# Fourteen weight units of layer 2 converted to float32 during layer 1, through scratch in device memory; eight late activations for twelve

## The chip, the cores and the metric

The kernel runs on one NeuronCore of a Trainium2 chip. The metric is device time in microseconds (us) of one execution, the median of several runs. The engines are named as the profile names them: TensorE is PE (its weight loads PEld), VectorE is DVE, ScalarE is ACT, GpSimd is POOL, SyncE is SP; ACT, POOL and SP also issue transfers.

## What is computed

The reference takes float32 inputs: an attention block whose heads are mixed before and after the softmax, and two dense layers. Only the layers matter here.

```python
# x: 896 tokens x 768, from the attention block
h = x @ w1_in                                  # 768 -> 2048
x = (h * clip(h + 3, 0, 6) / 6) @ w1_out       # 2048 -> 768
h = x @ w2_in                                  # 768 -> 2048
P = a0 + a1*h + a2*h**2 + a3*h**3
Q = 1 + |b0|*|h| + |b1|*h**2
out = (P / (Q + 1e-6)) @ w2_out                # 2048 -> 768
```

The weights of the layers arrive as 64-bit floats and have to be turned into 32-bit ones on the chip.

## The kernel before

Attention comes first (until about 262 us of the span); it isn't touched. The layers then work on weight units, in the order of the list `units`: 16 units `in1` (128 of the 2048 columns each), 18 units `out1`, and for layer 2 16 units `in2` and 16 `out2`, interleaved with `out2` one pass behind.

`load_unit` (L380) issues the load of a unit from SP into a tile `wraw` (two buffers): 768 KB for most. `split_pieces` (L394) then works in two halves. The first turns the 64-bit words into a float32 tile `wf` (two buffers; for `out2` a part of the large tile `wo2`): one ACT instruction (L408) for the high words and three DVE instructions on integers (L410, L412, L416). The second cuts the float32 into two float32r parts, `wh` and `wl` (three buffers each): in layer 1 both on POOL (L423, L424), in layer 2 `wh` on ACT (L426) and `wl` on DVE (L427). Every product is three matmuls (`mm3`, L364 to L366): high by high, high by low, low by high.

`advance(i)` (L446) loads units up to i+2 and splits units up to i+1. The code below the attention is written in the order of the units, and a scheduler moves instructions within it, engine by engine; each engine then runs its own list strictly in order.

Layer 1: for each f, two matmul groups (384 and 512 tokens, the two PARTS) into PSUM banks (eight, in turn), and `act1` (L506) on ACT and DVE, which writes `gh` and `gl`; its temporaries are the tiles `tmp` (seven buffers). Then, for each of six output column blocks, three `out1` units.

Layer 2, the main loop over f: 18 matmuls of 384 tokens into bank h0, `act2` (L701) on them, then 18 of 512 tokens into bank h1. `act2` is five ACT and six DVE instructions (L707, L710 to L714); bank h0 or h1 is free once L711 has read it. For most f the second part is "late": a copy on ACT (L759) takes it out of the bank, and its activation follows in the tail. `late_f` (L736) names these: twelve, all but f = 3, 7, 11, 15. `gemm_out0` adds 18 matmuls for the 384 tokens, one pass behind.

The tail is the output product of the 512 tokens, 16 steps of 24 matmuls, in the order `order` (L777): first the f that are not late, then the late ones. `prep(i)` (L780) makes the operands of a step: `gs` from the activation (ACT, and L719 on DVE) and `ws` from `wo2` (ACT L789, DVE L790). At step i the code writes down prep(i+2) and then the i-th late activation.

Of the kernel before, what the change touches and what calls it, by code (L numbers as in the profile page):

```python
# [7 lines left out]
F32 = mybir.dt.float32  # L8
F32R = mybir.dt.float32r
I32 = mybir.dt.int32  # L10
# [39 lines left out]
def fused_kernel(  # L50
# [15 lines left out]
    nc = tc.nc  # L66
    NT, DM = out.shape
    DFF = w1_out.shape[0]
    WARM = 11
    KD = DM // 128  # L70
    KF = DFF // 128
# [20 lines left out]
    w1i = w1_in.bitcast(I32).rearrange("(c p) f -> p c f", p=128)  # L92
    w1o = w1_out.bitcast(I32).rearrange("(f p) c -> p f c", p=128)
    w2i = w2_in.bitcast(I32).rearrange("(c p) f -> p c f", p=128)

    xp = tc.alloc_tile_pool(name="xp", bufs=1)
    x1p = tc.alloc_tile_pool(name="x1p", bufs=1)
# [263 lines left out]
    pools = {}  # L361
# [17 lines left out]

    def load_unit(u, eng=nc.sync):  # L380
        kind, i, kk = u
        t = pools['late'].tile([128, KD * 256], I32, tag="wraw", bufs=2, name="wraw")
        cols = slice(i * 256, i * 256 + 256)
        if kind in ("in1", "in2"):
            src = (w1i if kind == "in1" else w2i)[:, :, cols]
        elif kind == "out1":
            src = w1o[:, KSP[kk][0] : KSP[kk][1], cols]
        else:
            src = w2_out.bitcast(I32)[i * 128 : i * 128 + 128, :].rearrange("p (a b) -> p a b", b=256)
        n = src.shape[1]  # L390
        eng.dma_start(out=t[:, : n * 256].rearrange("p (a b) -> p a b", b=256), in_=src)
        raws[u] = (t, n)

    def split_pieces(u):  # L394


        t, n = raws.pop(u)
        n *= 128
        tv = t[:, : 2 * n].rearrange("p (a two) -> p a two", two=2)
        hw, lw = tv[:, :, 1], tv[:, :, 0]  # L400
        if u[0] == "out2":
            if not wo2:
                wo2.append(pools["gp2"].tile([128, KF, DM], F32, name="wo2"))
            w = wo2[0][:, u[1], :]
        else:
            w = pools["late"].tile([128, KD * 128], F32, tag="wf", bufs=2, name="wf")[:, :n]
        wi = w.bitcast(I32)
        nc.scalar.activation(out=w, in_=hw.bitcast(F32), func=AF.Copy, scale=2.0**-112)  # L408
        yield
# [7 lines left out]
            out=wi, in0=lw, scalar=icst[:, 1:2], in1=wi, op0=ALU.logical_shift_right, op1=ALU.bitwise_or  # L417
        )
        yield
        hv = pools["late"].tile([128, KD * 128], F32R, tag="wh", bufs=3, name="wh")[:, :n]  # L420
        lv = pools["late"].tile([128, KD * 128], F32R, tag="wl", bufs=3, name="wl")[:, :n]
        if u[0] in ("in1", "out1"):
# [78 lines left out]
            pass  # L501

    def tmp(name, n):
        return pools["gp"].tile([128, 512], F32, tag="tmp", bufs=7, name=name)[:, :n]

    def act1(f, p):  # L506
        t0, t1 = PARTS[p]
# [151 lines left out]
        return pm.tile([128, 512], F32, tag="mm", name=name)  # L659


    ui = 2
    for f in range(2, KF):
        advance(ui)
        for p in range(2):
            run(gemm1(f, p, bank(f"h1_{f}_{p}")))
            act1(f, p)
        ui += 1
    for c in range(KD):
        hp = [bank(f"y1_{c}_{p}") for p in range(2)]  # L670
        for kk, (k0, k1) in enumerate(KSP):
            advance(ui)
            wh, wl = spl.pop(("out1", c, kk))
            for f in range(k0, k1):
                for p, (t0, t1) in enumerate(PARTS):
                    mm3(hp[p][:, : t1 - t0], wh[:, f - k0, :], wl[:, f - k0, :], gh[f][:, t0:t1], gl[f][:, t0:t1],
                        f == 0, f == KF - 1)
            ui += 1
        for p, (t0, t1) in enumerate(PARTS):
            y = tmp("y", t1 - t0)  # L680
            nc.scalar.activation(out=y, in_=hp[p][:, : t1 - t0], func=AF.Copy, scale=1.0 / 6.0)
            nc.vector.tensor_copy(out=XH[:, c, t0:t1], in_=y)
            nc.vector.tensor_tensor(out=XL[:, c, t0:t1], in0=y, in1=XH[:, c, t0:t1].bitcast(F32), op=ALU.subtract)
# [49 lines left out]

    acc0 = []
    g0, g1 = {}, {}
    late_f = [f for f in range(KF) if f % 4 != 3]  # L736

    def gemm_out0(f):
        w = spl.pop(("out2", f, 0))
# [137 lines left out]
```

## Time and profile before

| | |
|---|---|
| time, median of 3 runs | 751.38 us (749.64 to 752.59) |
| the profiled execution | 750.68 us |
| its span, first to last instruction | 749.0 us |
| PE busy | 715.0 us, 95% of the span |
| DVE busy | 533.2 us, 71% |
| ACT busy | 427.9 us, 57% |
| POOL busy | 258.0 us, 34% |
| mean clock granted to PE | 0.986 of full speed |

The times of single instructions come from one profiled execution. Its span leaves out 1.7 us around the first and the last instruction. A busy PE is not PE at its peak: matmuls overlap, and a wait shorter than a matmul's length shows in the distance between starts and not as idle time. So the starts of PE's rows are of more use than its busy share.

### The profile page before, as it was taken

How to read it: one execution, taken by the hardware profiler on the slowest of the kernel's cores; microseconds unless marked ns; L12 is line 12 of the kernel's file. 1: busy time of each engine (PE TensorE's matmuls, PEld its weight loads, DVE VectorE, ACT ScalarE, POOL GpSimd, SP SyncE). 2: the span in 40 equal slices, each digit the busy share in tenths (PEclk: the TensorE clock that was granted, in tenths of full speed). 3: DMA queues.
4: the chain of work that ended last, by engine and by line, in shares of the span. 5: the costliest groups of instructions: out<-in, count | busy, mean ns of one | idle time of the engine just before them, and what ended most of it. 6: DMA issues, size and time to landing. Idle time of an engine off the chain costs nothing.

```text
span 749.0 us, 12177 instructions
## 1 busy us (share of the span) xinstructions
PE 715.0 (95%) x4457; PEld 621.4 (83%) x4457; DVE 533.2 (71%) x947; ACT 427.9 (57%) x869; POOL 258.0 (34%) x255
## 2 busy tenths in 40 slices
PE   5799999999998999999999999999999998999986
PEld 3578777787886988888888888889998897999876
DVE  5554556555456489767635555589999999999996
ACT  4577677777678444343411111256766575789872
POOL 1676766676668535444344333200000000000000
PEclk8899999999999999999999999999999999999999
DMA  6535356445358325333233333324354443501002
GB/s 187 176 122 155 119 179 183 142 141 149 118 151 227 99 85 167 91 122 106 93 113 112 111 97 94 121 85 132 122 169 127 126 144 110 169 18 46 1 1 84
DMA packets 63283, 89.76 MB, mean 120 GB/s; under 512 B 5172, under 2 KB 53880, under 8 KB 63224
## 3 DMA queue, kind: packets, MB, share of 16 engines
q1 hardware_dynamic: 62592, 88.55, 38.4%
q8 instruction: 35, 0.57, 0.3%
q10 hardware_dynamic: 568, 0.43, 0.2%
q14 instruction: 24, 0.20, 0.1%
q0 software_dynamic: 64, 0.01, 0.1%
HBM read 66.87 MB, written 2.75 MB: 93 GB/s over the span
## 4 chain that ended last, share of the span: by engine, by line
PE 74%; DVE 15%; ACT 4%; DMA 4%; issue 2%; SPq 1%; POOL 0%; ACTq 0%; POOLq 0%; DVEq 0%
PE h L364 9%; PE h L366 9%; PE h L365 9%; PE A L320 8%; PE X L340 5%; PE y L364 5%; PE y L365 5%; PE y L366 5%; PE sc L254 5%; PE M L285 4%; PE M L287 2%; PE acc L365 2%; PE M L286 2%; PE acc L366 2%; PE acc L364 2%
## 5 line engine op out<-in xcount | busy, mean ns | idle before, releaser
L364 PE MATMUL h<-xh,wh 128*128 128x512 f32 (+1 forms) x384 | 142.6, 371 | 2.3 <-DVE u L711 1.3
L366 PE MATMUL h<-xh,wl 128*128 128x512 f32 (+1 forms) x384 | 141.5, 370 | 2.1 <-DVE wl L427 2.1
L365 PE MATMUL h<-xl,wh 128*128 128x512 f32 (+1 forms) x384 | 141.3, 368 | 0.0
L408 ACT ACTIVATE wf<-wraw 128x768 f32<-128x768 f32 (+1 forms) x50 | 43.7, 875 | 122.8 <-POOL wl L424 101.4
L275 POOL TENSOR_TENSOR sl<-full,sh 120x448 fp32r<-120x448 f32 x89 | 103.5, 1163 | 7.4
L289 DVE TENSOR_REDUCE st<-M 120x1 f32<-120x448 f32 x90 | 56.1, 623 | 68.0 <-PE M L287 63.9
L320 PEld LDWEIGHTS A<-wr,e 120*112 120x112 f32 x720 | 85.1, 176 | 19.6 <-ACT wr L304 16.1
L320 PE MATMUL A<-wr,e 120*112 120x120 f32 x720 | 90.3, 268 | 8.4 <-ACT wr L304 8.1
L291 ACT ACTIVATE e<-M,st 120x448 f32<-120x448 f32 x90 | 57.1, 635 | 60.6 <-DVE st L289 60.5
L364 PEld LDWEIGHTS h<-xh,wh 128*128 128x128 f32 x384 | 72.6, 189 | 12.2 <-DVE u L711 2.2
L366 PEld LDWEIGHTS h<-xh,wl 128*128 128x128 f32 x384 | 72.5, 189 | 11.8 <-DVE wl L427 3.3
L273 POOL TENSOR_SCALAR sh<-full 120x448 fp32r<-120x448 f32 x89 | 54.1, 607 | 77.3 <-PE M L286 43.0
L410 DVE TENSOR_SCALAR wf<-wf 128x768 int32<-128x768 int32 (+1 forms) x50 | 27.6, 551 | 74.2 <-ACT wf L408 74.0
L365 PEld LDWEIGHTS h<-xl,wh 128*128 128x128 f32 x384 | 72.7, 189 | 8.2
L423 POOL TENSOR_SCALAR wh<-wf 128x768 fp32r<-128x768 f32 (+1 forms) x34 | 33.4, 982 | 128.8 <-PE y L365 56.0
L364 PE MATMUL y<-gh,wh 128*128 128x384 f32 x192 | 70.6, 368 | 0.0
L365 PE MATMUL y<-gl,wh 128*128 128x384 f32 x192 | 70.2, 366 | 0.0
L366 PE MATMUL y<-gh,wl 128*128 128x384 f32 x192 | 69.7, 363 | 0.0
L424 POOL TENSOR_TENSOR wl<-wf,wh 128x768 fp32r<-128x768 f32 (+1 forms) x34 | 65.7, 1934 | 2.8
L324 ACT ACTIVATE at<-A 112x480 f32<-112x480 f32 x90 | 51.5, 572 | 2.8 <-PE A L320 2.8
L416 DVE SCALAR_TENSOR_TENSOR wf<-wraw,icst,wf 128x768 int32<-128x768 int32 (+1 forms) x50 | 51.3, 1028 | 0.8
L412 DVE SCALAR_TENSOR_TENSOR wf<-wraw,icst,wf 128x768 int32<-128x768 int32 (+1 forms) x50 | 50.6, 1012 | 0.8
(113 smaller groups left out, 1515.7 us busy)
## 6 DMA issues: line engine op xcount, KB each, us to landing
wraw<-in_moe_w_in_dram SPq DMA_DIRECT2D x32, 768.0 KB
wraw<-in_moe_w_out_dram SPq DMA_DIRECT2D x28, 768.0 KB
full<-stg SPq DMA_DIRECT2D x60, 210.0 KB
vraw<-in_v_dram SPq DMA_DIRECT2D x42, 224.0 KB
full<-stg SPq DMA_DIRECT2D x24, 157.5 KB
wraw<-in_moe_w_out_dram SPq DMA_DIRECT2D x6, 512.0 KB
kraw<-in_k_dram SPq DMA_DIRECT2D x6, 448.0 KB
qraw<-in_q_dram SPq DMA_DIRECT2D x6, 360.0 KB
```

What stands on the lines that cost most here:

```text
L273: eng.tensor_scalar(out=sh[:r], in0=s[:r], scalar1=1.0, scalar2=0.0, op0=ALU.mult, op1=ALU.add)
L275: return eng.tensor_tensor(out=sl[:r], in0=s[:r], in1=sh[:r].bitcast(F32), op=ALU.subtract)
L289: nc.vector.tensor_reduce(out=st[:r, 0:1], in_=mt[:r, :S], op=ALU.max, axis=AX.X, negate=True)
L291: nc.scalar.activation(out=e[:r], in_=mt[:r, :S], func=AF.Exp, bias=st[:r, 0:1], accum_out=st[:r, 1:2])
L320: nc.tensor.matmul(av[:, jc], lhsT=e[:r, jc * JP : (jc + 1) * JP], rhs=wr[:r, :, :rr], start=True, stop=True)
L324: lambda: nc.scalar.activation(out=at[C][:, :, :, c0 : c0 + rr], in_=av, func=AF.Copy)
L364: nc.tensor.matmul(o, lhsT=wh, rhs=mh, start=first, stop=False)
L365: nc.tensor.matmul(o, lhsT=wh, rhs=ml, start=False, stop=False)
L366: nc.tensor.matmul(o, lhsT=wl, rhs=mh, start=False, stop=last)
L412: nc.vector.scalar_tensor_tensor(out=wi, in0=hw, scalar=icst[:, 0:1], in1=wi, op0=ALU.bitwise_and, op1=ALU.bitwise_or)
L416: nc.vector.scalar_tensor_tensor(out=wi, in0=lw, scalar=icst[:, 1:2], in1=wi, op0=ALU.logical_shift_right, op1=ALU.bitwise_or)
L424: nc.gpsimd.tensor_tensor(out=lv, in0=w, in1=hv.bitcast(F32), op=ALU.subtract)
```

## The change

The units `in2` of f = 2 to 15 get their first half (`to_f32`, the same four instructions) during layer 1. A function `pre_slot` is called after each f of layer 1 and after each `out1` unit, 32 times. It takes two calls for a unit: the first loads the 64-bit unit into a tile `wpre` (one buffer), the second converts it into a `wf` buffer; the first call for the next unit, ahead of its own load, stores the `wf` to a scratch tensor `pre` in device memory. All these transfers are issued by SP. In layer 2 `load_unit` reads the float32 back (384 KB) straight into a `wf` buffer, and `split_pieces` only does its second half. The room for `wpre` comes from `tmp`, four buffers for seven. And `late_f` becomes the eight even f, so that eight second activations run in the loop where four did, and eight follow in the tail where twelve did. The order of the tail's steps changes with it: f = 1, 3, ... 15, then 0, 2, ... 14. Everything computed is the same.

```diff
@@ -92,6 +92,11 @@
+    PRE2 = list(range(2, KF))
+    dram = ctx.enter_context(tc.tile_pool(name="dram", bufs=1, space=bass.MemoryType.DRAM))
+    pre = {f: dram.tile([128, KD * 128], F32, name=f"pre{f}") for f in PRE2}
@@ -379,6 +384,11 @@
     def load_unit(u, eng=nc.sync):
         kind, i, kk = u
+        if kind == "in2" and i in pre:
+            t = pools["late"].tile([128, KD * 128], F32, tag="wf", bufs=2, name="wf")
+            eng.dma_start(out=t, in_=pre[i])
+            raws[u] = (t, KD)
+            return
@@ -391,19 +401,11 @@
-    def split_pieces(u):
...
+    def to_f32(t, n, w):
...
         wi = w.bitcast(I32)
         nc.scalar.activation(out=w, in_=hw.bitcast(F32), func=AF.Copy, scale=2.0**-112)
         yield
...
@@ -417,6 +419,20 @@
+    def split_pieces(u):
+        t, n = raws.pop(u)
+        n *= 128
+        if u[0] == "in2" and u[1] in pre:
+            w = t
+        else:
+            if u[0] == "out2":
+                if not wo2:
+                    wo2.append(pools["gp2"].tile([128, KF, DM], F32, name="wo2"))
+                w = wo2[0][:, u[1], :]
+            else:
+                w = pools["late"].tile([128, KD * 128], F32, tag="wf", bufs=2, name="wf")[:, :n]
+            yield from to_f32(t, n, w)
@@ -501,7 +517,7 @@
     def tmp(name, n):
-        return pools["gp"].tile([128, 512], F32, tag="tmp", bufs=7, name=name)[:, :n]
+        return pools["gp"].tile([128, 512], F32, tag="tmp", bufs=4, name=name)[:, :n]
@@ -659,12 +675,35 @@
+    slot, held = [0], {}
+
+    def pre_slot():
+        i, k = divmod(slot[0], 2)
+        slot[0] += 1
+        if k == 0 and 0 < i <= len(PRE2):
+            nc.sync.dma_start(out=pre[PRE2[i - 1]], in_=held["w"])
+        if i >= len(PRE2):
+            return
+        f = PRE2[i]
+        n = KD * 128
+        if k == 0:
+            held["t"] = gp.tile([128, 2 * n], I32, tag="wpre", name=f"wpre{f}")
+            nc.sync.dma_start(
+                out=held["t"].rearrange("p (a b) -> p a b", b=256), in_=w2i[:, :, f * 256 : f * 256 + 256]
+            )
+        else:
+            held["w"] = pools["late"].tile([128, n], F32, tag="wf", bufs=2, name="wf")
+            for _ in to_f32(held["t"], n, held["w"]):
+                pass
     ui = 2
     for f in range(2, KF):
         advance(ui)
         for p in range(2):
             run(gemm1(f, p, bank(f"h1_{f}_{p}")))
             act1(f, p)
+        pre_slot()
         ui += 1
...
+            pre_slot()
             ui += 1
@@ -733,7 +773,7 @@
-    late_f = [f for f in range(KF) if f % 4 != 3]
+    late_f = [f for f in range(KF) if f % 2 == 0]
```

The lists of the engines move at three places. The first is DVE in layer 1, around the activation of f=8. In the names, g1, t1, gh8 and gl8 belong to `act1`, h1_8_0 is the first matmul group of f=8, and wf is a unit under conversion. Before:

```order
L516 SCALAR_TENSOR_TENSOR g1_3952<-t1_3950,h1_8_0_3929 128x384
L416 SCALAR_TENSOR_TENSOR wf_4109<-wraw_4044,icst_68,wf_4109 128x768
L519 TENSOR_TENSOR gl8_3949<-g1_3952,gh8_3948 128x384
L516 SCALAR_TENSOR_TENSOR g1_3977<-t1_3975,h1_8_1_3956 128x512
L410 TENSOR_SCALAR wf_4172<-wf_4172 128x768
L519 TENSOR_TENSOR gl8_3949<-g1_3977,gh8_3948 128x512
L412 SCALAR_TENSOR_TENSOR wf_4172<-wraw_4107,icst_68,wf_4172 128x768
L516 SCALAR_TENSOR_TENSOR g1_4015<-t1_4013,h1_9_0_3992 128x384
L416 SCALAR_TENSOR_TENSOR wf_4172<-wraw_4107,icst_68,wf_4172 128x768
```

The same place with the change:

```order
L532 SCALAR_TENSOR_TENSOR g1_3991<-t1_3989,h1_8_0_3968 128x384
L418 SCALAR_TENSOR_TENSOR wf_4093<-wraw_4023,icst_68,wf_4093 128x768
L535 TENSOR_TENSOR gl8_3988<-g1_3991,gh8_3987 128x384
L412 TENSOR_SCALAR wf_4159<-wf_4159 128x768
L414 SCALAR_TENSOR_TENSOR wf_4159<-wraw_4091,icst_68,wf_4159 128x768
L418 SCALAR_TENSOR_TENSOR wf_4159<-wraw_4091,icst_68,wf_4159 128x768
L532 SCALAR_TENSOR_TENSOR g1_4016<-t1_4014,h1_8_1_3995 128x512
L412 TENSOR_SCALAR wf_4220<-wf_4220 128x768
L414 SCALAR_TENSOR_TENSOR wf_4220<-wpre6_4155,icst_68,wf_4220 128x768
L535 TENSOR_TENSOR gl8_3988<-g1_4016,gh8_3987 128x512
L532 SCALAR_TENSOR_TENSOR g1_4057<-t1_4055,h1_9_0_4034 128x384
L418 SCALAR_TENSOR_TENSOR wf_4220<-wpre6_4155,icst_68,wf_4220 128x768
```

The three instructions on wf_4220 are the unit f=6 of `in2`, converted from wpre; around it stand the activations and the conversions of layer 1's own units.

The second place is DVE in the loop of layer 2, at f=9. Here t1, y0, u and r belong to `act2`, g0l9 is the split of its result, wo2 a unit `out2` under conversion, h2_9_0 and h2_9_1 the contents of banks h0 and h1. Before:

```order
L713 SCALAR_TENSOR_TENSOR u_6193<-u_6193,pa_66,r_6196 128x384
L410 TENSOR_SCALAR wo2_5337<-wo2_5337 128x768
L714 SCALAR_TENSOR_TENSOR t1_6192<-y0_6194,u_6193 128x384
L427 TENSOR_TENSOR wl_6240<-wf_6234,wh_6239 128x768
L719 TENSOR_TENSOR g0l9_6209<-t1_6192,g0h9_6208 128x384
L412 SCALAR_TENSOR_TENSOR wo2_5337<-wraw_6232,icst_68,wo2_5337 128x768
L416 SCALAR_TENSOR_TENSOR wo2_5337<-wraw_6232,icst_68,wo2_5337 128x768
L410 TENSOR_SCALAR wf_6333<-wf_6333 128x768
L412 SCALAR_TENSOR_TENSOR wf_6333<-wraw_6261,icst_68,wf_6333 128x768
L427 TENSOR_TENSOR wl_6268<-wo2_5337,wh_6267 128x768
```

With the change:

```order
L751 SCALAR_TENSOR_TENSOR u_6309<-u_6309,pa_66,h2_9_0_6289 128x384
L412 TENSOR_SCALAR wo2_5465<-wo2_5465 128x768
L752 SCALAR_TENSOR_TENSOR y0_6310<-y0_6310,r_6312 128x384
L753 SCALAR_TENSOR_TENSOR u_6309<-u_6309,pa_66,r_6312 128x384
L414 SCALAR_TENSOR_TENSOR wo2_5465<-wraw_6658,icst_68,wo2_5465 128x768
L754 SCALAR_TENSOR_TENSOR t1_6308<-y0_6310,u_6309 128x384
L443 TENSOR_TENSOR wl_6393<-wo2_5465,wh_6392 128x768
L747 SCALAR_TENSOR_TENSOR y0_6348<-h2_6349,pb_67,y0_6348 128x512
L759 TENSOR_TENSOR g0l9_6325<-t1_6308,g0h9_6324 128x384
L750 TENSOR_TENSOR u_6347<-h2_9_1_6328,u_6347 128x512
L418 SCALAR_TENSOR_TENSOR wo2_5465<-wraw_6658,icst_68,wo2_5465 128x768
L751 SCALAR_TENSOR_TENSOR u_6347<-u_6347,pa_66,h2_9_1_6328 128x512
```

The conversion of wf is gone, and the second activation of f=9 (on h2_9_1, 512 columns) stands in its place; its third instruction, L751 on h2_9_1, is the one that frees bank h1.

The third place is DVE at the end of the late activations in the tail. The xl rows from wo2 and from g1 are the two DVE instructions of a preparation, the others the activation of f=13 and f=14. Before:

```order
L713 SCALAR_TENSOR_TENSOR u_7360<-u_7360,pa_66,r_7363 128x512
L790 TENSOR_TENSOR xl_85<-wo2_5337,xh_84 128x768
L714 SCALAR_TENSOR_TENSOR g1_13_6582<-y0_7361,u_7360 128x512
L707 SCALAR_TENSOR_TENSOR y0_7404<-h2_7405,pb_67,y0_7404 128x512
L710 TENSOR_TENSOR u_7403<-g1_14_6681,u_7403 128x512
L719 TENSOR_TENSOR xl_85<-g1_13_6582,xh_84 128x512
L711 SCALAR_TENSOR_TENSOR u_7403<-u_7403,pa_66,g1_14_6681 128x512
L712 SCALAR_TENSOR_TENSOR y0_7404<-y0_7404,r_7406 128x512
L713 SCALAR_TENSOR_TENSOR u_7403<-u_7403,pa_66,r_7406 128x512
L790 TENSOR_TENSOR xl_85<-wo2_5337,xh_84 128x768
L714 SCALAR_TENSOR_TENSOR g1_14_6681<-y0_7404,u_7403 128x512
```

With the change:

```order
L747 SCALAR_TENSOR_TENSOR y0_7346<-h2_7347,pb_67,y0_7346 128x512
L750 TENSOR_TENSOR u_7345<-g1_14_6800,u_7345 128x512
L759 TENSOR_TENSOR xl_101<-g1_4_5790,xh_100 128x512
L751 SCALAR_TENSOR_TENSOR u_7345<-u_7345,pa_66,g1_14_6800 128x512
L752 SCALAR_TENSOR_TENSOR y0_7346<-y0_7346,r_7348 128x512
L753 SCALAR_TENSOR_TENSOR u_7345<-u_7345,pa_66,r_7348 128x512
L830 TENSOR_TENSOR xl_101<-wo2_5465,xh_100 128x768
L754 SCALAR_TENSOR_TENSOR g1_14_6800<-y0_7346,u_7345 128x512
L759 TENSOR_TENSOR xl_101<-g1_6_5992,xh_100 128x512
L830 TENSOR_TENSOR xl_101<-wo2_5465,xh_100 128x768
```

Before, the last activation, of f=14, is interleaved with the preparation of step 14 (f=13). With the change it is interleaved with that of step 10 (f=4), and behind it stand preparations alone, the first of them that of step 11 (f=6).

PE's list keeps its order but for neighbours, and POOL's is the same. SP's list gains 14 loads into wpre and 14 stores of wf, each store directly ahead of the next wpre load and behind two loads of layer 1.

## Rows read from the trace of the kernel before

**Rows 1.** The page: engines over the whole span, and DVE by fortieths of it.

```profile
PE 715.0 (95%) x4457; PEld 621.4 (83%) x4457; DVE 533.2 (71%) x947; ACT 427.9 (57%) x869; POOL 258.0 (34%) x255
...
DVE  5554556555456489767635555589999999999996
```

**Rows 2.** Busy time by stretch: us, then PE, PEld, DVE, ACT, POOL, PEclk, DMA, GB/s.

```profile
262.00:380.00 118.00, 118.00 (x573) 104.33 (x573) 90.67 (x118) 51.00 (x83) 50.20 (x32) 1.00 0.36 110
380.00:492.00 112.00, 112.00 (x552) 99.98 (x551) 57.22 (x72) 20.59 (x29) 40.90 (x30) 1.00 0.35 110
492.00:669.00 177.00, 172.64 (x868) 156.80 (x867) 170.16 (x258) 119.17 (x194) 0.00 (x0) 0.99 0.39 121
669.00:745.00 76.00, 70.82 (x384) 67.43 (x382) 72.03 (x110) 57.81 (x95) 0.00 (x0) 0.98 0.08 31
```

**Rows 3.** Timeline of PE: first matmuls of f=0, 4, 7 and of the tail.

```profile
492.27 0.34 PE L364 MATMUL h<-xh,wh 128*128 128x384 f32 x1
...
542.07 0.34 PE L364 MATMUL h<-xh,wh 128*128 128x384 f32 x1
...
573.71 0.34 PE L364 MATMUL h<-xh,wh 128*128 128x384 f32 x1
...
668.80 0.51 PE L364 MATMUL acc<-xh 128*128 128x384 f32 x2
```

**Rows 4.** Waits of PE, loop (492 to 669), then tail: total, times, longest.

```profile
PE h L366 <- DVE wl L427: 2.1, 2, 1.6
PE h L364 <- DVE u L711: 1.3, 2, 1.0
...
PE acc L365 <- DVE xl L790: 4.1, 3, 2.2
```

**Rows 5.** Groups of DVE by shape, 492 to 745: busy us, mean ns, idle before.

```profile
L416 DVE SCALAR_TENSOR_TENSOR wo<-wraw,icst,wo 128x768 int32<-128x768 int32 x16 | 16.2, 1014 | 0.1
...
L707 DVE SCALAR_TENSOR_TENSOR y<-h,pb,y 128x512 f32<-128x512 f32 x16 | 11.9, 745 | 0.0
L712 DVE SCALAR_TENSOR_TENSOR y<-y,r 128x512 f32<-128x512 f32 x16 | 11.0, 685 | 0.1
...
L410 DVE TENSOR_SCALAR wo<-wo 128x768 int32<-128x768 int32 x16 | 8.9, 554 | 0.2 <-ACT wo L408 0.2
```

**Rows 6.** Timeline of DVE in the tail: L707 rows two steps apart.

```profile
695.68 0.74 DVE L707 SCALAR_TENSOR_TENSOR y<-h,pb,y 128x512 f32<-128x512 f32 x1
...
706.22 0.74 DVE L707 SCALAR_TENSOR_TENSOR y<-h,pb,y 128x512 f32<-128x512 f32 x1
```

**Rows 7.** Timeline of DVE in the tail: preparation 3's end, and the last copy.

```profile
677.15 0.95 DVE L790 TENSOR_TENSOR xl<-wo,xh 128x768 fp32r<-128x768 f32 x1
...
745.11 0.56 DVE L730 COPY o<-acc 128x384 f32<-128x384 f32 x1 [1.24 <-PE acc L366]
```

**Rows 8.** Waits of POOL, 262 to 492: total us, times, longest.

```profile
POOL wh L423 <- PE y L365: 56.0, 15, 5.0
POOL wh L423 <- PE h L365: 52.2, 13, 4.4
```

**Rows 9.** Timeline of POOL in layer 1: one unit's split.

```profile
301.35 1.40 POOL L423 TENSOR_SCALAR wh<-wf 128x768 fp32r<-128x768 f32 x1 [4.02 <-PE h L365]
302.83 2.04 POOL L424 TENSOR_TENSOR wl<-wf,wh 128x768 fp32r<-128x768 f32 x1
```

**Rows 10.** Timeline: a load issued by SP, and ACT's first use of it.

```profile
497.31 0.37 SPq L391 DMA_DIRECT2D wraw<-in_moe_w_in_dram  x1
...
501.94 0.92 ACT L408 ACTIVATE wf<-wraw 128x768 f32<-128x768 f32 x1 [0.97 <-DMA wraw<-in_moe_w_in_dram]
```

**Rows 11.** Groups of DVE by shape, 262 to 492; last row 492 to 745.

```profile
L416 DVE SCALAR_TENSOR_TENSOR wf<-wraw,icst,wf 128x768 int32<-128x768 int32 x28 | 29.7, 1065 | 0.5
...
L519 DVE TENSOR_TENSOR gl<-g,gh 128x384 fp32r<-128x384 f32 x16 | 19.4, 1211 | 0.6 <-ACT gh L518 0.6
...
L719 DVE TENSOR_TENSOR g0l<-t,g0h 128x384 fp32r<-128x384 f32 x16 | 8.8, 553 | 1.6 <-ACT g0h L718 1.6
```

More of the change, by code (lines that the diff above doesn't have):

```diff
@@ L392, in load_unit @@
         raws[u] = (t, n)
-    def split_pieces(u):
-        t, n = raws.pop(u)
-        n *= 128
+    def to_f32(t, n, w):
         tv = t[:, : 2 * n].rearrange("p (a two) -> p a two", two=2)
         hw, lw = tv[:, :, 1], tv[:, :, 0]
[L401 to L406, printed above, removed]
         wi = w.bitcast(I32)
```

## Prediction

> **What bounds the kernel now.** I read the page first, then a table of busy time by stage, then TensorE's own rows in layer 2, then what it waits for there. On the page TensorE (PE) is busy 95% of the span and VectorE (DVE) 71%, but the DVE slices show that its work is uneven: mostly four to seven tenths, nine from slice 28 (506 us) on [rows 1]. The table by stage says where that matters [rows 2]. From 262 to 492 us (layer 1 without its first units) PE is busy in every microsecond, DVE for 90.7 of 118 us and then for 57.2 of 112, GpSimd (POOL) for 50.2 and 40.9. From 492 to 669 (the main loop of layer 2) DVE is busy 170.2 of 177 us and PE 172.6; from 669 to 745 (the tail) DVE has 72.0 of 76 and PE 70.8. POOL does nothing in either. So layer 1 is bound by PE with DVE time to spare, and in layer 2 both engines are full and PE begins to wait.
>
> How much PE loses there comes from its cadence. Pass f=4 starts at 542.07 and pass f=7 at 573.71, so an undisturbed pass takes 31.64/3 = 10.55 us. Sixteen would take 168.8, but the loop takes 668.80 - 492.27 = 176.5 [rows 3]: a loss of 7.7 us. A pass is 36 matmuls of 384 columns and 18 of 512; shared out by columns, one of 384 costs 0.176 us. The tail's 384 matmuls would then take 67.5 us; from 668.80 to the last copy out of PSUM at 745.11 it takes 76.3 [rows 3, 7]: a loss of 8.8. The longest waits of PE name DVE: its weight split, its u product and, in the tail, its xl split [rows 4]. They add up to 7.5 us, less than the 16.5 lost, in part because a stall also costs clock: 0.99 and 0.98 of full speed were granted in loop and tail, 1.00 before [rows 2].
>
> **The change, part by part.** *Conversions leave layer 2.* A unit is three DVE instructions, L410 of 0.55 us and two of 1.01 (L416 stands for both) [rows 5], 2.58 us by durations; in a row each starts up to 0.08 us before the end of the one in front, so 2.3 to 2.6. Of the fourteen units thirteen are converted inside the loop now and one just ahead of it. Thirteen at 2.4 take 31 us from DVE in the loop. ScalarE (ACT) loses one instruction a unit as well, which I cost at nothing: PE's waits hardly name it.
>
> *Four late activations come into the loop.* An activation of 512 columns is six DVE instructions, three like L707 and three like L712 [rows 5], 4.29 us by durations. Their pitch is read in the tail, where L707 rows two steps apart are 10.54 us apart [rows 6]: 5.27 us a step, for an activation (3.8) and a preparation (1.47, two instructions). Four add 15 us to the loop. DVE's load there becomes 170.2 - 31 + 15 = 154 us against 168.8 of PE, 91%, so PE sets the loop. In a pass with odd f, though, DVE has some 11.3 us of work against PE's 10.55; in an even one 7.5. The second order excerpt shows what is tight: in f=9 the u product that frees PSUM bank h1 now stands in DVE's row behind the whole first activation and pieces of a conversion. From the end of h2_9_0 I count some 1.1 us for ACT's readings, fourteen instructions of together 8.6 us, and 0.8 of waits for ACT: 10.5. The bank is wanted after 18 matmuls of 512 columns, 4.2 us, and 36 of 384, 6.3: also 10.5. I add 1 us for such touches over eight odd passes: 169.8.
>
> *The tail.* DVE needs 16 preparations and 8 activations, 16 x 1.47 + 8 x 3.8 = 54 us, against 67.5 of PE, but the order counts (third excerpt): an activation stands between two preparations until the eight are through, so that a step costs DVE 5.27 us and PE 24 x 0.176 = 4.22. Preparation 3 starts its last instruction at 677.15 and ends 9.2 us into the tail [rows 7]; as many instructions stand ahead of it after the change. From there to the end of preparation 10 are 7 preparations and 7.3 activations, 10.3 + 27.7 = 38.0 us: it is ready 47.2 us in, while PE would reach step 10 at 42.2. Behind it only preparations follow, and PE runs its last six steps freely: 47.2 + 6 x 4.22 = 72.5. A part of step 10 doesn't need the last piece; I take 72.0 in place of 76.3. What is late next is thus still DVE, for some 4.5 us.
>
> *Layer 1 receives the work*: fourteen conversions, seven in each stage. DVE goes to 109 of 118 us (92%) and to 75 of 112. I cost this at nothing; the cover is the lead of the weights. POOL's split of a unit waits for PE, 108 us in 28 waits [rows 8]; with three buffers it then has two units in hand, 14.7 us in the first stage (a unit is 18 matmuls of each width), less its own 3.5 [rows 9]: 11.2 us. Eight PSUM banks let the activations lag by four units. If the cover is gone, each microsecond of lag is one of PE.
>
> *A wait is added on the wf ring and in SP's queue.* The two wf buffers now also hold a converted unit until it is stored. A unit behind it on the ring waits for that store, and in SP's queue the loads behind the store wait for its conversion. Over four units of the first stage (29.5 us) the longest round is three conversions, which I estimate at 4.5 us each with the work between their pieces, and two POOL splits of 3.5: 20.5 us, which leaves 9 for issue and landing of one store. The trace has no such store in the middle. From below it costs nothing; the nearest rows are the last output, 192 KB, copied by 745.67 and landed by the end of the span at 749.0, 3.3 us [rows 1, 7], and a 768 KB load, issued at 497.31 and used at 501.94, 4.6 us [rows 10]. I take 4, between them as its size is: hidden.
>
> *Loads in layer 2* become 384 KB instead of 768, may be issued once the split two units of the same kind earlier is done, some 20 us ahead of use, and leave the two wraw buffers to the out units: hidden. *tmp from seven buffers to four* still holds two parts of an activation in flight: nothing.
>
> Sum: loop start 492.3, loop 169.8, tail 72.0, last copy and store 3.9 (745.11 to 749.0): 738.0 us of span. The profiled execution took 750.68 beside a span of 749.0, so 739.7, rounded to **739.5**: 11.2 less than that execution, which lies 0.7 below the median of 751.38.
>
> **The rivals.** *A. Bank h1 becomes the bound.* Eight passes instead of four hold it until u. For it: PE waited 1.3 us for u already, once for 1.0 [rows 4]. Against: DVE was full then. If each odd pass loses 1 us more: 747.5.
>
> *B. DVE and POOL block each other in layer 1.* There the gl split of 384 columns took 1.21 us on average; in layer 2, where POOL is idle, the like g0l took 0.55, a factor of 2.2. But the conversion's L416 took 1.07 against 1.01 [rows 5, 11]. If the moved instructions paid 2.2, the seven of the first stage would be 40 us and DVE would need 131 of 118: 13 us behind, of which the lead covers 11. That gives 742, and 752 if it covers nothing. The Trainium skill (SBUF — State Buffer, "Who interferes with whom") has a rule that speaks against the change: VectorE with two SBUF inputs, or in a two-port mode, and GpSimd lock each other out for whole instructions. By that rule it would be 742 to 752; the trace agrees for gl and hardly for L416.
>
> *C. The store chokes the ring (slower).* Where a store takes over 9 us, each further microsecond is lost once per round of four units, in some seven rounds. At 12 us that gives 739.5 + 21 = 760; it decides for slower from 11.2 us on. Against: no transfer in these rows takes half of that.
>
> *D. The conversions were not the bound of the loop*, but latencies between ACT, DVE and PE. Then only the tail gains: 746. If the tail doesn't either, nothing changes: 750.
>
> **How the numbers follow.** Forecast 0.75; A 0.09; B 0.06; C 0.04; D 0.06. The forecast's own range is 735 to 744 (no loss in loop and tail at all would be 734). A, most of B and of D lie up to 747.5, so the range is 734.5 to 747.5. A measurement of this kernel tells 0.5% from no change: 747.6 to 755.1 is the same. Faster 0.88, same 0.08, slower 0.04.
>
> **What would show it.** Right: POOL's waits in layer 1 still for PE; the first matmul of layer 2 still at 492; passes of 10.55 us throughout, with DVE near 90% in the loop; one stretch of stalls some 40 us into the tail, for xl, and none after it. Wrong: a first matmul of layer 2 later than 494 (B, or C if a conversion waits for a store ahead of POOL); u as what PE waits for in odd passes (A); a tail still of 76 us; or passes that still lengthen with DVE at 90% (D).

## The result, and the profile after

The changed kernel takes 757.86 us (median of five runs, 757.16 to 760.65), the kernel before 751.38 in the same five rounds: a ratio of 1.0099, 95% interval 1.0082 to 1.0116. It is **slower by 1.0%**, where 739.5 was forecast; the time lies outside the range of 734.5 to 747.5. The profiled execution took 757.86 beside a span of 756.2.

On the page PE keeps its share of 95% and DVE rises from 71% [rows 1] to 75%; the shares say nothing of the loss.

TensorE's own rows say at once where the time went. They are the first matmuls of f=0, 4 and 7 and of the tail, as in [rows 3]:

```profile
512.75 0.34 PE L369 MATMUL h<-xh,wh 128*128 128x384 f32 x1
...
562.34 0.34 PE L369 MATMUL h<-xh,wh 128*128 128x384 f32 x1
...
593.98 0.34 PE L369 MATMUL h<-xh,wh 128*128 128x384 f32 x1
...
681.53 0.34 PE L369 MATMUL acc<-xh 128*128 128x384 f32 x1
```

Layer 2 begins at 512.75 instead of 492.27: **20.5 us late**. From there all goes as forecast. Passes 4, 5 and 6 take 31.64 us, 10.55 each; the loop takes 681.53 - 512.75 = 168.8 (176.5 before). The last copy out of PSUM, the row answering to [rows 7], says when the tail ends:

```profile
752.32 0.56 DVE L770 COPY o<-acc 128x384 f32<-128x384 f32 x1 [1.58 <-PE acc L371]
```

The tail took 752.32 - 681.53 = 70.8 (76.3 before), and 3.9 follow to the end of the span. So layer 2 gained 13.3 us and layer 1 lost 20.5; the difference is the 7.2 us by which the span grew.

Some words for what follows: an early unit is one of the fourteen units of `in2` that are converted in layer 1; the in stage is the part of layer 1 that works on units `in1` (until about 380), the out stage the part that works on units `out1`; the wf ring is the two `wf` buffers, used in turn.

Busy time by stretch of the changed kernel, answering to [rows 2] (us, then PE, PEld, DVE, ACT, POOL, PEclk, DMA, GB/s); the stretches follow its own stages:

```profile
262.00:380.00 118.00, 115.54 (x565) 101.21 (x562) 106.71 (x119) 49.37 (x78) 41.59 (x28) 1.00 0.52 159
380.00:512.00 132.00, 122.04 (x569) 105.97 (x568) 100.50 (x111) 32.34 (x47) 48.35 (x34) 0.96 0.54 173
...
512.70:681.50 168.80, 168.80 (x865) 155.71 (x865) 155.96 (x243) 117.63 (x197) 0.00 (x0) 1.00 0.29 94
681.50:752.00 70.50, 67.49 (x386) 66.28 (x384) 56.60 (x86) 45.37 (x75) 0.00 (x0) 1.00 0.09 34
```

In the loop PE is busy in every microsecond with DVE at 156.0 of 168.8 (92%). In layer 1, where PE had no gap, it now stands idle 12.4 us, 10.0 of them after 380, where the granted clock is also 0.96 in the mean, a share of the time at the lower of its two levels. DVE is not full there (100.5 of 132). PE's waits in layer 1 (total us, times, longest) all name POOL:

```profile
PE y L371 <- POOL wl L440: 6.3, 4, 1.8
PE y L369 <- POOL wh L439: 3.5, 3, 1.9
PE h L371 <- POOL wl L440: 2.5, 2, 1.5
```

And POOL, which waited for PE in [rows 8] and so was ahead of it, now waits for DVE (262 to 512):

```profile
POOL wh L439 <- DVE wf L418: 137.7, 24, 11.9
POOL wh L439 <- PE y L370: 10.8, 1, 10.8
```

A step further back stands ACT. Its two longest waits in that stretch concern the wf ring:

```profile
ACT wf L410 <- POOL wl L440: 57.8, 18, 5.9
ACT wf L410 <- DMA pre<-wf: 47.6, 13, 8.8
```

The second is the wait that the change added: ACT, about to write a wf buffer, stands until the store of the early unit in it has landed. In layer 1 it is the only transfer that ACT waits for; no load ends a wait of ACT there. One turn in the in stage, from the chain of work that ended last (start, us, what):

```profile
306.08 2.48 DVE wf L414
...
309.62 0.94 DVE wf L418
...
310.58 4.63 DMA pre<-wf
...
316.08 0.58 ACT t L530
...
316.68 0.55 DVE g L532
317.24 0.63 DVE wf L418
```

The second of the conversion's three DVE pieces (L414) took 2.48 us; POOL's timeline shows what ran beside it:

```profile
305.71 2.03 POOL L440 TENSOR_TENSOR wl<-wf,wh 128x768 fp32r<-128x768 f32 x1
```

The early unit is finished at 310.56 and its store lands at 315.2. Behind the waiting conversion in ACT's row stands `t`, the first step of an activation; DVE's `g` waits for that `t`; and behind `g` in DVE's row stands the last piece (L418) of the *other* unit, whose own buffer was never in question. ACT's conversions of early units show the turn's length:

```profile
302.79 0.92 ACT L410 ACTIVATE wf<-wpre 128x768 f32<-128x768 f32 x1 [3.10 <-POOL wl L440]
...
315.29 0.89 ACT L410 ACTIVATE wf<-wraw 128x768 f32<-128x768 f32 x1 [3.00 <-DMA pre<-wf]
...
321.48 0.92 ACT L410 ACTIVATE wf<-wpre 128x768 f32<-128x768 f32 x1 [3.10 <-POOL wl L440]
...
338.25 0.91 ACT L410 ACTIVATE wf<-wpre 128x768 f32<-128x768 f32 x1 [3.10 <-POOL wl L440]
...
404.75 0.92 ACT L410 ACTIVATE wf<-wpre 128x768 f32<-128x768 f32 x1 [5.63 <-POOL wl L440]
412.85 1.46 ACT L410 ACTIVATE wf<-wraw 128x512 f32<-128x512 f32 x2 [7.18 <-DMA pre<-wf]
419.30 0.92 ACT L410 ACTIVATE wf<-wpre 128x768 f32<-128x768 f32 x1 [4.12 <-POOL wl L440]
```

From one early conversion to the next are 18.7 and 16.8 us in the in stage, where PE wants two units every 14.7. In the out stage it is 14.6 at 404.75, and 12.7 to 17.1 in the others, where PE's eighteen units in 112 us make 12.4 for two; there the conversions of two units can stand behind one store (412.85, x2). That is the theory the experiments started from: **the added wait closes a cycle through ACT's row** (conversion, store, conversion and split of the units behind it, next conversion). The rivals: DVE and POOL stretch each other's instructions (rival B), DVE has no room at all, or the stores' traffic slows the loads.

### The profile page after: what moved, and what is told of

It is laid out like the page before. It is cut to its first block, busy times and chain, and to the rows that moved or that the text cites. A ratio compares the mean times of both kernels' runs of the same rounds, so it can differ in the third digit from the quotient of the medians.

```text
span 756.2 us, 12264 instructions
## 1 busy us (share of the span) xinstructions
PE 715.7 (95%) x4457; PEld 622.3 (82%) x4457; DVE 563.6 (75%) x947; ACT 424.1 (56%) x865; POOL 256.1 (34%) x255
## 4 chain that ended last, share of the span: by engine, by line
PE 57%; DVE 25%; DMA 6%; ACT 5%; issue 3%; POOL 3%; SPq 0%; ACTq 0%; POOLq 0%; DVEq 0%
PE A L325 8%; DVE wf L414 6%; PE h L371 5%; PE h L369 5%; PE h L370 5%; PE X L345 5%; PE sc L259 4%; DMA pre<-wf 4%; PE M L290 4%; DVE wf L418 3%; PE acc L370 3%; PE acc L371 3%; PE acc L369 3%; DVE wf L412 3%; PE y L371 2%
## 5 line engine op out<-in xcount | busy, mean ns | idle before, releaser
L325 PEld LDWEIGHTS A<-wr,e 120*112 120x112 f32 x720 | 85.2, 176 | 19.7 <-ACT wr L309 16.1
L371 PE MATMUL y<-gh,wl 128*128 128x384 f32 x192 | 72.2, 376 | 6.5 <-POOL wl L440 6.3
L369 PE MATMUL y<-gh,wh 128*128 128x384 f32 x192 | 72.6, 378 | 3.5 <-POOL wh L439 3.5
L370 PE MATMUL y<-gl,wh 128*128 128x384 f32 x192 | 71.9, 374 | 0.0
L410 ACT ACTIVATE wf<-wraw 128x768 f32<-128x768 f32 (+1 forms) x36 | 30.8, 866 | 65.4 <-DMA pre<-wf 47.6
L412 DVE TENSOR_SCALAR wf<-wf 128x768 int32<-128x768 int32 (+1 forms) x50 | 38.0, 760 | 26.7 <-ACT wf L410 26.7
L290 PE MATMUL M<-sh,wp_h 120*120 120x448 f32 x90 | 41.9, 466 | 8.4 <-DVE sh L278 8.4
L414 DVE SCALAR_TENSOR_TENSOR wf<-wraw,icst,wf 128x768 int32<-128x768 int32 (+1 forms) x36 | 47.8, 1326 | 0.7
```

The lines of the kernel that those rows point to most:

```text
L290: nc.tensor.matmul(mt[:r, :S], lhsT=a[:r, :r], rhs=sh[:r], start=True, stop=False)
L325: nc.tensor.matmul(av[:, jc], lhsT=e[:r, jc * JP : (jc + 1) * JP], rhs=wr[:r, :, :rr], start=True, stop=True)
L369: nc.tensor.matmul(o, lhsT=wh, rhs=mh, start=first, stop=False)
L370: nc.tensor.matmul(o, lhsT=wh, rhs=ml, start=False, stop=False)
L371: nc.tensor.matmul(o, lhsT=wl, rhs=mh, start=False, stop=last)
L412: nc.vector.tensor_scalar(out=wi, in0=wi, scalar1=3, scalar2=None, op0=ALU.logical_shift_left)
```

## Experiments

### The wait, the traffic, the buffer

**One store instead of fourteen.**

```diff
-            eng.dma_start(out=t, in_=pre[i])
+            eng.dma_start(out=t, in_=pre[2])
...
-        if k == 0 and 0 < i <= len(PRE2):
+        if k == 0 and i == 1:
```

> The changed kernel with one store instead of fourteen: only the first early unit is stored, and all fourteen loads of layer 2 read that one, so the kernel leaves out thirteen stores and computes layer 2 with repeated weights. The ring keeps its three turns per pair. If the store's 4.7 us are what closes the cycle, a period of 16.8 to 18.7 us falls to about 13 and PE sets 14.7: start of layer 2 at 493 to 498, time 738 to 743. If sharing two buffers among three turns is enough without the store, the start lies at 500 to 508, time 745 to 753. Theory port or load: start above 508, time above 753.

Measured: 737.70 us, 0.9813 of before (0.9793 to 0.9834). Layer 2 begins at 494.28. So 18.5 of the 20.5 us come from the stores, by their wait or by their traffic; the conversions themselves cost layer 1 at most the 2 us by which this start lies behind the 492.27 of before.

**The stores without the wait.**

```diff
-            nc.sync.dma_start(out=pre[PRE2[i - 1]], in_=held["w"])
+            nc.sync.dma_start(out=pre[PRE2[i - 1]], in_=XL[:, KD - 1, : KD * 128].bitcast(F32))
```

> The changed kernel with its fourteen stores kept in size, number and place, but reading another tile that was finished long before (a part of xl), so that a wf buffer waits for no store; layer 2 then computes with those values in place of its weights. The run without thirteen stores took away the wait and the traffic at once; this one takes away the wait alone. Theory wait: nearly all of the 20 us comes back. With the traffic kept, loads land later than without stores (6.2 us against 4.4 for 768 KB in the runs so far), which the two raw buffers cover: layer 2 begins at 493 to 498, the time is 737 to 743. Rival traffic (5.4 MB of stores slow the loads that ACT waits for): the start stays above 508, the time above 752. Between the two, the share of each is read from the start.

Measured: 738.17 us, 0.9824 (0.9794 to 0.9854). Start of layer 2, and the whole of layer 1 by engines, in this run:

```profile
494.52 0.34 PE L369 MATMUL h<-xh,wh 128*128 128x384 f32 x1
```

```profile
262.00:494.00 232.00, 232.00 (x1159) 205.47 (x1156) 211.89 (x229) 81.13 (x125) 91.18 (x62) 1.00 0.56 177
```

The 20 us are back here too (0.5 us more than with one store, with ranges that overlap). But the stores did not keep their place. With nothing to wait for, SP issued all fourteen of them early, the first and the last of them here:

```profile
255.40 0.96 SPq L685 DMA_DIRECT2D pre<-xl  x2
...
289.92 1.33 SPq L685 DMA_DIRECT2D pre<-xl  x1
```

In the changed kernel they are issued from 279.62 to 485.27, and PE waits for POOL for the first time at 355.08. So this run shows that the conversions cost PE nothing when no buffer waits for a store; what the traffic costs where it fell in the changed kernel it does not show. Against the traffic as the cause speaks the changed kernel's own trace, in which no load ends a wait of ACT in layer 1, while the stores end 47.6 us; the next experiment keeps the stores spread over layer 1 and takes away the wait.

The row also bears on rivals B and load. DVE is busy 211.9 of 232 us, and the pieces of a conversion are long beside POOL, as its groups in layer 1 show (busy, mean ns, idle before):

```profile
L414 DVE SCALAR_TENSOR_TENSOR wf<-wraw,icst,wf 128x768 int32<-128x768 int32 x27 | 39.6, 1468 | 0.6
...
L414 DVE SCALAR_TENSOR_TENSOR wf<-wpre,icst,wf 128x768 int32<-128x768 int32 x14 | 20.9, 1496 | 0.2
```

The same instruction (L412 there) took 1.02 us before, and still PE is busy in all 232 us:

```profile
L412 DVE SCALAR_TENSOR_TENSOR wf<-wraw,icst,wf 128x768 int32<-128x768 int32 x28 | 28.5, 1018 | 0.4
```

POOL waits for DVE here too, but in time. The Trainium skill (SBUF — State Buffer, "Who interferes with whom") has a DVE instruction with two SBUF inputs and a GpSimd instruction that reads SBUF lock each other out of a shared port pair; the lengthened pieces agree with it. So neither the lengthening nor DVE's load costs time by itself. That the lengthening adds to the loss where the wait is there too is another matter, taken up below.

**A buffer of its own for the early unit** (tmp from four buffers to two, for room), and as its control two tmp buffers alone:

```diff
-            held["w"] = pools["late"].tile([128, n], F32, tag="wf", bufs=2, name="wf")
+            held["w"] = gp.tile([128, n], F32, tag="wfp", name=f"wfp{f}")
...
-        return pools["gp"].tile([128, 512], F32, tag="tmp", bufs=4, name=name)[:, :n]
+        return pools["gp"].tile([128, 512], F32, tag="tmp", bufs=2, name=name)[:, :n]
```

> The fourteen early units get an SBUF buffer of their own, outside the wf ring (tmp goes from four buffers to two to make room). Theory ring: the changed kernel lost its 20.5 us in layer 1 because two wf buffers serve three turns per pair of units, and because ACT's next conversion waits for a store in a row that also holds the activations. With the wait gone the first matmul of layer 2 returns to 492 to 496 us (512.75 now, 492.27 before), layer 2 keeps its passes of 10.55 us, and the time is 737 to 742. Theory port (DVE and POOL stretch each other, so that a conversion costs DVE 7.8 us instead of 4.5): the start stays above 505, the time above 750. Theory load (DVE has no room in layer 1 at all): the start stays near 512, the time near 757. Were two tmp buffers too few, DVE's row would show waits for tmp in both layers.

> The control for the two experiments with an own buffer: the changed kernel with two tmp buffers instead of four, nothing else. If two hold enough, the time stays at that of the changed kernel, 756.5 to 759.5. If tmp were short, ACT's activations would wait for DVE's last reading of them, and it would be slower, 760 or more. If it were faster by more than 2 us, own_t2's gain would not be the ring's.

Measured: 746.24 us with the own buffer, 0.9935 (0.9910 to 0.9959); layer 2 begins at 500.60. The control took 760.87, 1.0128 (1.0105 to 1.0150), some 3 us more than the changed kernel by the medians and more than the 756.5 to 759.5 expected: two tmp buffers are a little short there. So the gain of 11.6 us is the buffer's and not the tmp's. With the fourteen stores still spread over layer 1, **taking the wait off the ring is worth 12 of the 20.5 us.** The lengthening of the pieces falls with it: L414 of an early unit takes 1.25 us in the mean here, 1.83 in the changed kernel (262 to 500). But no theory had 500.60: 8 us stayed. What ACT waits for in the out stage (380 to 500) is no longer the store but the raw load of the next early unit, with the following conversions queued behind:

```profile
ACT wfp L410 <- DMA wpre<-in_moe_w_in_dram: 40.8, 6, 12.7
```

### The remainder

**Load ahead of store**, on the own buffer and on the ring:

```diff
-        if k == 0 and 0 < i <= len(PRE2):
-            nc.sync.dma_start(out=pre[PRE2[i - 1]], in_=held["w"])
...
             nc.sync.dma_start(
                 out=held["t"].rearrange("p (a b) -> p a b", b=256), in_=w2i[:, :, f * 256 : f * 256 + 256]
             )
+            store()
```

> As own_t2, but the raw load of the next early unit is issued ahead of the store of the last one. In own_t2 layer 2 began at 500.60, 8 us late; its one long stall (1.97 and 1.61 us at 457) was POOL behind ACT, which stood 12.7 us before a conversion whose raw data landed 6.2 us after its issue, right behind the store. Theory chain: conversion, store, load and the next conversion form a cycle of some 14 us against 12.4 that PE takes for two units in the out stage. With the load in front, it lands 1.5 to 2.5 us earlier: the cycle falls to 12 to 13, the stall to under 1 us, layer 2 begins at 493 to 497, the time is 739 to 743. Rival (the wait was for DVE's share, not for the load): the start stays at 499 to 502 and the time at 745 to 747.

> The changed kernel with that order alone, load ahead of store, still on the wf ring. Theory ring: the store now lands behind a 768 KB load, 2 to 4 us later, and ACT's next conversion waits that much longer in each of 14 turns: the start of layer 2 goes from 512.75 to 520 to 545, the time to 765 to 790. If the early load's landing were what chokes layer 1 in the changed kernel too, the start would move forward to 500 to 510, and the time below 755.

Both expectations missed. On the own buffer it took 748.67 us, 0.9964 (0.9949 to 0.9979), no better than the order before. ACT merely waits for the other transfer (own buffer, load first, 380 to 505):

```profile
ACT wfp L410 <- DMA pre<-wfp: 49.5, 6, 12.9
```

Store and load leave the queue within 0.5 us of each other, and whichever is second lands some 6 us later: issued 443.53, landed by 449.7 with the store first; 435.26 and 441.2 with the load first. The next conversion needs both.

On the ring it took 755.47, 1.0059 (1.0041 to 1.0077): 2.4 us *less* than the changed kernel, where 765 or more was expected. The store does land later, 5.9 to 6.4 us after its issue (issued 280.75, 296.78 and 312.92), but now the early conversion follows the delayed one at once, its buffer having been split during the wait. ACT's conversions of this run:

```profile
286.69 0.89 ACT L410 ACTIVATE wf<-wraw 128x768 f32<-128x768 f32 x1 [3.30 <-DMA pre<-wf]
288.00 0.90 ACT L410 ACTIVATE wf<-wpre 128x768 f32<-128x768 f32 x1
...
302.72 0.90 ACT L410 ACTIVATE wf<-wraw 128x768 f32<-128x768 f32 x1 [2.48 <-DMA pre<-wf]
304.09 0.90 ACT L410 ACTIVATE wf<-wpre 128x768 f32<-128x768 f32 x1
```

The turn is 16.1 us, with a longer store in it, against 16.8 to 18.7. So the store's length does not set the turn by itself; what else has become serial with it does.

**One early unit per three units in the out stage**, thirteen in all (`PRE2` ends at KF - 1), on the own buffer and on the ring (four tmp buffers):

```diff
-            pre_slot()
+            if kk != 1:
+                pre_slot()
             ui += 1
+        if c == KD - 1:
+            pre_slot()
```

> own_t2 (own buffer, store ahead of load again, eight late activations), but in layer 1's out stage an early unit is converted in every third unit's slot instead of every second one, thirteen early units in all. In own_t2 and in own_ls ACT stood before the next early conversion until the second of the two transfers had landed, 6 us after their issue, whichever was second; from one early conversion's start on ACT to the next took up to 14.8 us, where PE needs 12.4 for two units of the out stage, and 14.7 in the in stage. Theory chain (conversion, transfers, conversion): at one in three units PE takes 18.7 us, more than the chain, so PE's waits for POOL at 457 go and layer 2 begins at 492.5 to 496 (500.60 in own_t2); the one unit that layer 2 converts again costs nothing there. Time 738 to 741. Rival (the early units are too much for DVE and ACT in the out stage by their mere work): a thirteenth less work changes little, start 498 to 501, time 744 to 747.

> The changed kernel on its wf ring with four tmp buffers, with that cadence alone: every third slot in the out stage, thirteen early units. In the changed kernel the ring's period was 16.8 to 18.7 us in the in stage (PE 14.7) and 12.7 to 17.1 in the out stage (PE 12.4). Theory ring: the out stage, at 18.7 us for three units, no longer loses, the in stage still falls behind by some 2.5 us in each of seven rounds, 17 us, of which the lead covers 11: layer 2 begins at 497 to 502, time 742 to 748. If the out stage's stalls have another cause than the period, the start stays above 508 and the time above 752.

On the own buffer: **739.60 us, 0.9844 (0.9820 to 0.9868)**, as expected; layer 2 begins at 493.12. PE's waits for POOL are gone; layer 1 and the loop of this run:

```profile
262.00:493.00 231.00, 230.63 (x1126) 204.56 (x1126) 190.42 (x225) 79.64 (x124) 91.91 (x62) 1.00 0.56 176
493.00:662.00 169.00, 169.00 (x867) 155.89 (x866) 158.17 (x246) 119.06 (x199) 0.00 (x0) 1.00 0.30 96
```

That fits the chain theory of the remainder; the run changes the cadence and drops one unit, and the two were not tried apart.

On the ring it missed: 760.97 us, 1.0125 (1.0102 to 1.0148), where 742 to 748 was expected. Layer 2 does begin at 509.93, 2.8 us earlier than in the changed kernel, where 497 to 502 was expected; but its loop takes 174.5 us instead of 168.8, with a wait for the last split of y in its first pass and a granted clock of 0.89 until 540:

```profile
PE h L369 <- DVE xh L725: 2.9, 1, 2.9
```

In layer 1, with more time per turn the turn simply became longer. Its chain in the out stage, one turn of it:

```profile
408.35 4.42 DMA wraw<-in_moe_w_out_dram
...
412.88 0.95 ACT wf L410
...
418.15 2.33 DVE xl L726
...
422.04 1.03 DVE wf L418
...
423.09 2.73 DMA pre<-wf
...
425.93 0.90 ACT wf L410
...
428.72 1.02 DVE wf L418
...
429.80 4.32 DMA wraw<-in_moe_w_out_dram
```

From load to load are 21.5 us, all serial: a load (it could not be issued before ACT and DVE had freed a wraw buffer), a unit's conversion, the split of the output y (xh and xl), the early conversion, the store, the next unit's conversion, which frees wraw for the next load. While ACT stands before the store, SP's loads stand too, and the lead that the loads had is lost. PE needs 18.7. My expectation had taken the turn for a fixed length that only needed more room.

### The late activations

**The conversions alone** (twelve late activations as before) and **the late activations alone** (kernel before, eight late):

```diff
-    late_f = [f for f in range(KF) if f % 2 == 0]
+    late_f = [f for f in range(KF) if f % 4 != 3]
```

> The changed kernel with the twelve late activations of before; only the early conversions remain of the change. Layer 1 should not care: start of layer 2 at 512 to 513. In the loop DVE has some 15 us less to do and PE sets the same 168.8. In the tail DVE has four activations more: by the prediction's step of 5.27 against 4.22 us, twelve activations hold preparation 14 until 15.6 x 1.47 + 12 x 3.8 = 68 us into the tail, so the tail takes 74 to 76 instead of 70.8. Time 761 to 763. If the tail were freed by something else than the count of late activations, the time would stay at 758.

```diff
-    late_f = [f for f in range(KF) if f % 4 != 3]
+    late_f = [f for f in range(KF) if f % 2 == 0]
```

> The kernel before with only eight late activations; nothing is converted early. Layer 1 as before: start of layer 2 at 492.3. DVE had 170.2 of 177 us of the loop; with four activations of 3.8 to 4.3 us more it has 185 to 187, so the loop becomes DVE's and takes 186 to 189 instead of 176.5; the tail takes 70 to 72 instead of 76.3. Sum 755 to 762: the late activations can't be brought in without taking the conversions out. If the loop's stalls were latencies and not DVE's load, the loop stays near 177 and the time falls to 746.

Conversions alone: 763.91 us, 1.0161 (1.0141 to 1.0181). Layer 2 begins at 514.81, with the loss of layer 1 in it. In the loop DVE falls to 143.1 of 169 us and PE is never idle; from the loop's end (682.85) the last matmul starts 75.3 us later, at 758.14 (70.4 us in the changed kernel), with waits for xl. Late activations alone: 768.42 us, 1.0223 (1.0202 to 1.0244), more than expected. Its loop and the waits of PE in it:

```profile
493.00:692.00 199.00, 179.79 (x864) 160.72 (x863) 184.96 (x281) 129.07 (x209) 0.00 (x0) 0.96 0.34 108
```

```profile
PE h L364 <- ACT wh L426: 16.7, 8, 3.9
PE h L366 <- DVE wl L427: 2.3, 4, 0.7
```

DVE had 185 us of work, as expected, but the loop took 199 (493.48 to 692.60) where 186 to 189 was expected: with DVE at 93%, weights that come late cost stalls of up to 4 us each and clock (0.96). So each half has its own gain: the conversions alone bring the loop to 168.0 us (176.5 before) and leave the tail near its 76, the activations alone bring the tail to 71.1 and lengthen the loop. Moving the conversions makes the room that the activations take.

**Six late activations** on own_ls and on own3:

```diff
-    late_f = [f for f in range(KF) if f % 2 == 0]
+    late_f = [f for f in range(KF) if f % 2 == 0 and f % 8 != 6]
```

> own_ls with six late activations instead of eight. In the changed kernel's tail PE still waits 3.0 us for xl, at steps 7 to 9, where eight activations stand between the preparations. With six DVE is 2 x 5.27 - 2 x 1.47 = 7.6 us ahead there and the three waits should go; the loop gets 8 to 9 us of DVE work more, 164 of 169 us. If DVE still keeps up, 3 us less than own_ls (736 to 740). If the loop is DVE's again, its stalls return, with wh and wl as what PE waits for: the time of own_ls or up to 4 us more.

> own3 with six late activations. own_ls6 took 3.3 us less than own_ls, with DVE at 172.5 of 180 us and no wait of PE in the loop. Here DVE converts one unit more in the loop, 2.4 us, which brings it to 97%. If it still keeps up: 735.5 to 738, 3 us less than own3. If that is too much: PE waits for wh or wl in the last passes, and the time is that of own3 or up to 3 us more.

Measured: 745.41 us on own_ls, 0.9923 (0.9904 to 0.9942), 3.3 less than own_ls. Not all of that is the activations': its layer 2 also began earlier (502.37 against 505.66). From there to the last matmul it took 236.6 us against 239.1 in the profiled executions, so some 2.5 us are theirs. On own3 it is **736.45 us, 0.9805 (0.9785 to 0.9825)**, the best of all, 3.2 less than with eight late. Its layer 2 began 1.2 us later (494.29); from there to the last matmul it took 237.1 us against 239.2. DVE is busy 164.2 of 169 us in the loop, and one wait of PE for xl is left in layer 2, 0.8 us:

```profile
494.00:663.00 169.00, 168.90 (x867) 155.45 (x867) 164.19 (x258) 124.39 (x206) 0.00 (x0) 1.00 0.30 96
```

## Why the prediction was wrong, by its steps

- *The loop* (169.8): right, 168.8, with no wait of PE at all. Rivals A and D fall: u ends no wait, and the loop is PE's once the conversions are out.
- *The tail* (72.0): right, 70.8. It has one stretch of three waits for xl, 3.0 us, the first at 717.84, 36 us into the tail, and none after; "some 40 us in" was forecast. DVE's price for the conversions (31 us) and for the four activations (15) is borne out in the main: late12 has 27 us less of DVE in the loop than the kernel before, before8 15 more.
- *Layer 1 receives the work, at nothing*: right for the work itself. With the wait gone, fourteen conversions more leave layer 2 at 494.3 to 494.5 instead of 492.3, part of it the programs' own starts (before8, whose layer 1 is the old one, begins at 493.48). DVE's price was too low: 36 us (14 of 2.58) were put, and it pays 211.9 - 149.5 = 62, the 149.5 being its busy time of before over the same 262 to 494. The rest is pieces that became longer, the unmoved ones too.
- ***A wait is added on the wf ring and in SP's queue*, hidden**: this step failed, and with it the start of the loop (492.3 against 512.75). The store's size held: 2.8 to 4.7 us against the 4 taken. The conversion's did not: 4.5 was put, and an early one took 7.8 in the in stage, with L414 at 2.48. Nor did the structure. I counted one longest round over four units, 20.5 of 29.5 us, which left 9 for the store. The trace shows a turn from one early conversion to the next, in two units of PE's time: conversion 7.8 us in the in stage (302.79 to 310.56) and 5.2 in the out stage, store 4.7 and 2.8, then the conversion and split of the other unit, 6.2 and 6.5. These make 18.7 of 14.7 available, and 14.6 of 12.4. The step looked behind the store in SP's queue and along the ring, but **not behind the waiting conversion in ACT's row**, where the activations and the other unit's conversion stand. The lead of 11 us was then spent, and PE lost the rest. How much of the loss is structure and how much the long conversion stays open: with 4.5 us for it the usual turn of the in stage, 16.8, would be 13.5, less than PE's 14.7. That is an estimate from these rows; no run kept the wait and took away the lengthening. In the out stage, where it took 5.2, the turns were still too long.
- *Rival C*, the store that chokes the ring, was the right mechanism with the wrong condition: it was to decide only from a store of 11.2 us, and got 0.04. *Rival B* costs nothing by itself: in the run with the stores out of the way the pieces lengthen by half and PE has no gap. In the changed kernel the lengthened pieces stand on the turn that the wait has made serial, and there they count.
- *tmp from seven buffers to four, at nothing*: seven against four was not tried; two against four cost some 3 us on the ring, by the medians.

With the wait gone and the cadence that fits, own3 has 493.1 for the start, 168.8 for the loop and 70.8 for the tail: a span of 736.8 where the sum had 738.0. That its median of 739.60 agrees with the forecast to 0.1 us is in part luck; the step on the ring is what separates 757.9 from it.

## What to carry to other kernels

When a change adds a wait to an instruction, list what stands behind it on *its own engine*, and for each of those what stands behind whoever waits for it: here a store of 3 to 5 us stopped an activation, that an unrelated conversion, and that POOL. A cycle is costed as the sum of everything that has become serial in one turn, against the time that the bound engine takes for the same turn; a lead in front of it only delays the loss. Work that is moved to an engine with room can be free (62 us of DVE cost PE at most 2). A conversion's price is read beside the engines that it will run beside, for what is free off the turn counts in full on it. The buffer that the work borrows is not free: give it one of its own, and set its cadence by conversion plus transfers.

## What the runs showed of the hardware

- The DVE piece L414 of 768 columns, 1.02 us in the mean of layer 1 before, took 2.48 where it ran beside POOL's `wl` (306.08 above). In the run with the stores out of the way it took 1.5 us in the mean of layer 1, and PE, busy in all 232 us, lost nothing by it.
- A store of 384 KB with a load of 768 KB issued within 0.5 us behind it landed in 2.8 to 4.7 us (the changed kernel); the second of the two landed some 6 us after its issue, whichever it was (own_t2, own_ls).
- Fourteen stores of 384 KB that nothing waited for, issued from 255.4 to 289.9, left the time within 0.5 us of that with one store, whose in stage moves 149 GB/s (262 to 380). What they cost spread over layer 1, with nothing waiting, was not measured.
